# Attention and feed-forward on one core: two score groups per step, first transposes on TensorE, loads in smaller pieces and another order

## The chip, the core and the metric

The kernel runs on one core of a Trainium2 chip. The core has TensorE (PE; its weight loads are shown as PEld), VectorE (DVE), ScalarE (ACT), GpSimd (POOL) and SyncE (SP), and 16 DMA engines that all queues share. The metric is the device time of one execution in microseconds (us): the median of the runs, lower is better. The profile comes from one execution of its own.

## What is computed

Causal attention over 8 batches and 8 heads (S = 576 tokens, head size 64), with 16 extra "beacon" keys and values per head that every token may see; then a feed-forward layer without a nonlinearity on all 4608 tokens. Inputs and output are float32.

```python
k_all = concat([beacon_k, k], axis=2); v_all = concat([beacon_v, v], axis=2)
scores = q @ k_all.T / sqrt(64)              # causal mask on the non-beacon keys
a = softmax(scores);  attn = a @ v_all       # per batch and head
x = attn with heads side by side             # 4608 x 512
out = (((x @ w1) * (x @ w2)) @ w3) @ w_out   # w1, w2: 512x1024; w3: 1024x1024; w_out: 1024x512
```

## The kernel before

**Data.** All operands are float16 in SBUF; the loads on POOL's queue convert from float32. q, k and v of one batch come in five pieces of up to 128 tokens (`load_q`, `load_k`, `load_v`; the first piece of k and v holds the beacons) into two sets of buffers (batch number modulo 2). q and k are transposed by DMA transposes on SP's queue (`transpose_qk`, two per piece), so that the head dimension lies on the partitions. w3 and w_out are multiplied once into one matrix `Wt` (`fuse`), since nothing nonlinear lies between them; for it w3 is loaded into the unused second half of the buffer `xT` and transposed by eight DMA transposes on SP.

**Attention.** The unit is a pair of heads of one batch (32 pairs in all). Scores are computed transposed, keys on partitions, tokens on columns, and the causal upper part is left out. The blocks of a pair are packed into four groups of 368, 512, 384 and 400 columns per head (`GROUPS`), each for both heads in one PSUM tile `ps` of two banks; two such tiles exist. One step of the main loop (128 steps, 16 per batch) treats one group: `scores` on PE and the exponential on ACT straight into `pT`, `mask` on DVE (groups 0, 2 and 3), `values` on PE: p times v with a column of ones for the sum, then reciprocal and multiplication on DVE into `x16`. Values of token tiles 0 and 1 follow group 0, tiles 2 and 3 follow group 2, tile 4 follows group 3 (`DONE`). The scores run two steps ahead of the values. With the last pair of a batch each finished tile of `x16` goes through a DMA transpose on SP (line 326) into `xT`.

**Feed-forward.** Nine blocks of 512 tokens. `ff_ab` makes, for each of eight slices of 128 hidden units, two sums of four matmuls: the first is copied by ACT (`a_sb`, line 198), the second is multiplied with it on DVE (`gT`, line 200). `ff_out` multiplies gT with Wt, four sums of eight matmuls, which DVE scales (line 218) and SP stores. All PSUM tiles `pm` come from three banks. `stream` strings this together as a generator that gives one matmul at a time: block 0's `ff_ab`, then `fuse`, then `ff_out`, then the other blocks; 928 matmuls in all.

**Order.** Written by hand; every engine runs its own instructions in program order and waits by semaphores. Ahead of the loop: memsets, the mask constants, then on POOL's queue the loads of batch 0 (q, k, v), of w1 and w2 (2 DMAs), batch 1, w3 (4 DMAs), w_out; on SP's queue the transposes of batch 0, batch 1 and w3. In the loop each step issues scores(s+2), from step 20 on its share of FF matmuls (`emit_ff`), mask(s+1) and values(s). The first five steps of batch b issue the loads of batch b+1, steps 4 to 8 its transposes. What is left of the FF stream, 232 matmuls, follows the loop.

Of the kernel before, what the change touches and what calls it, by code (L numbers as in the profile page):

```python
# [23 lines left out]
GW = [368, 512, 384, 400]  # L24
GO = [400, 768, 1280, 0]
PW = 1664
# [11 lines left out]
DONE = [[0, 1], [], [2, 3], [4]]  # L38


@with_exitstack
def kernel(
# [13 lines left out]
    nc = tc.nc  # L56
# [19 lines left out]
    w3T = const.tile([P, NFT, DF], FP16, name="w3T")  # L76
# [11 lines left out]
    gp = ctx.enter_context(tc.tile_pool(name="gp", bufs=2))  # L88
    asb = ctx.enter_context(tc.tile_pool(name="asb", bufs=3))
# [6 lines left out]


    for i in range(NB2):
        nc.vector.memset(k16s[i][64:128, 4, :], 0.0)
        nc.vector.memset(vas[i][64:128, 4, :, :], 0.0)  # L100
    for m in (MA, MB):
        nc.gpsimd.memset(m, 1.0)
    for m, base in (
        (MA[:, 0:128], 0),
        (MA[:, 128:240], Nb),
        (MB[:, 0:128], 0),
        (MB[:, 128:256], 0),
    ):
        nc.gpsimd.affine_select(
            m,  # L110
            m,
            pattern=[[1, m.shape[1]]],
            compare_op=ALU.is_ge,
            fill=0.0,
            base=base,
            channel_multiplier=-1,
        )
    for i in range(NB2):
        for jt in range(NJT):
            n = P if jt < 4 else S + Nb - 4 * P  # L120
            nc.vector.memset(vas[i][0:n, jt, :, 64:65], 1.0)


    def load_q(b, c):
        rows = min(P, S - c * P)
        nc.gpsimd.dma_start(  # L126
            q16s[b % NB2][:rows, c, :].rearrange("s (h d) -> s h d", h=H),
            q[b, :, ds(c * P, rows), :].rearrange("h s d -> s h d"),
        )
# [23 lines left out]
    for c in range(NJT):  # L153
        load_q(0, c)
        load_k(0, c)
        transpose_qk(0, c)
    for c in range(NJT):
        load_v(0, c)
    for i, w in enumerate((moe_w1, moe_w2)):
        nc.gpsimd.dma_start(  # L160
            w12[:, :, ds(i * DF, DF)], w.rearrange("(t p) f -> p t f", p=P)
        )
    for c in range(NJT):
        load_q(1, c)
        load_k(1, c)
        transpose_qk(1, c)
# [3 lines left out]
    w316 = xT[:, :, ds(M // 2, 2 * DF)].rearrange("p a (c r) -> p a c r", c=2)  # L170
    for a in range(NKT):
        nc.gpsimd.dma_start(
            w316[:, a], moe_w3[ds(a * 2 * P, 2 * P)].rearrange("(c p) r -> p c r", p=P)
        )
    nc.gpsimd.dma_start(wo16, moe_w_out.rearrange("(t p) n -> p t n", p=P))
# [46 lines left out]
    def fuse():  # L222
        for kt in range(NFT):
            pm = psM.tile([P, DM], FP32, name="pm")
            for rt in range(NFT):
                nc.tensor.matmul(  # L226
                    pm,
                    w3T[:, rt, ts(kt, P)],
                    wo16[:, rt, :],
                    start=(rt == 0),  # L230
                    stop=(rt == NFT - 1),
                )
                if rt < NFT - 1:
                    yield
            nc.scalar.copy(Wt[:, kt, :], pm)
            yield
# [11 lines left out]
    def emit_ff(upto):  # L248
        nonlocal emitted
        while emitted < upto:  # L250
# [7 lines left out]
    NS = B * NT * 4  # L258
    pTs, pss, x16s = {}, {}, {}

    def scores(s):
        b, t, g = s // (4 * NT), (s // 4) % NT, s % 4
        if g == 0:
            pTs[s // 4] = ptp.tile([P, 2, PW], FP16, name="pT")
        ps = psS.tile([P, 2, 512], FP32, name="ps")
        pT = pTs[s // 4]
        qT, kT = qTs[b % NB2], kTs[b % NB2]
        for jt, q0, n, col in GROUPS[g]:
            for hh in range(2):
                nc.tensor.matmul(  # L270
                    ps[:, hh, ds(col, n)],
                    kT[ds(hh * 64, 64), t, ts(jt, P)],
                    qT[ds(hh * 64, 64), t, ds(q0, n)],
                )
        nc.scalar.activation(  # L275
            pT[:, :, ds(GO[g], GW[g])], ps[:, :, 0 : GW[g]], AF.Exp, scale=scale
        )

    def mask(s):
        g = s % 4  # L280
        pT = pTs[s // 4]
        if g == 1:
            return
        m = {0: MA, 2: MB, 3: MB[:, 0:80]}[g]
        n = m.shape[1]
        blk = pT[:, :, ds(GO[g], n)]
        nc.vector.tensor_tensor(  # L287
            blk, blk, m.unsqueeze(1).to_broadcast([P, 2, n]), ALU.mult
        )

    def values(s):
        b, t, g = s // (4 * NT), (s // 4) % NT, s % 4
        tiles = DONE[g]
        if not tiles:
            return
        pT = pTs[s // 4]
        va = vas[b % NB2]
        if t == 0 and g == 0:
            x16s[b] = xp.tile([P, NJT, DM], FP16, name="x16")
        x16 = x16s[b]  # L300
        ni = len(tiles)
        pv = psV.tile([P, 4, VS], FP32, name="pv")
# [10 lines left out]
        rd = sm.tile([P, 4], FP32, name="rd")  # L313
# [16 lines left out]
    S0 = 20  # L330
    FF_END = 7 * 96 + 64 - 40
    scores(0)
    scores(1)
    mask(0)
# [47 lines left out]
```

## Time and profile before

| | |
|---|---|
| runs | 377.56 us median of 3 (377.11 to 381.39) |
| profiled execution | 379.91 us, span 378.2 us |
| PE busy | 289.4 us, 77% of the span, 2592 matmuls |
| ACT, DVE, POOL busy | 155.6, 153.1, 115.9 us |
| PE busy in 0 to 100 us | 21.6 us |
| DMA | 46.31 MB, mean 122 GB/s |
| DMA queues' packet time, share of 16 engines' span | POOL's loads 72.9%, SP's transposes and stores 41.8% |

How to read the lines in the prediction. A line of the timeline or of the chain begins with its start and its length in us, then engine, line of the kernel, operation, output and input tiles, "x6" for six instructions merged, and in brackets the idle time before it and what ended that. A line of a group gives count, busy time in us and mean ns of one, then the idle time ahead of the group. Matmuls overlap and their ends are modelled, so a matmul's cost in a dense stretch is read from start to start, not from its length. In the rows of 40 slices a digit is the busy share of the slice in tenths. A DMA issue's line ends with the KB of each and the median us from issue to landing. PE at work does not always run at the same pace, though the granted clock is 1.00 in every stage of this profile: the durations show it.

### The profile page before, as it was taken

The page shows a single profiled execution, that of the slowest core. Times are in us where ns is not written, and L with a number is a line of the kernel's source. Part 1 is how long each engine was busy: PE and PEld are TensorE (multiplying, and loading weights), DVE is VectorE, ACT ScalarE, POOL GpSimd, SP SyncE. Part 2 cuts the span into 40 slices and gives each one's busy share as a digit, 9 for nine tenths or more (in the row PEclk, how much of TensorE's full clock was granted, in tenths as well). Part 3 has the DMA queues.
Part 4 walks back from the last instruction along what each step waited for, and adds up shares of the span by engine and source line. Part 5 has one row for each costly group of instructions (what it writes and reads, how often), then busy time and mean ns, then how long its engine had stood idle before and what let it go on. Part 6 is the DMA issues. An engine that isn't in the chain of part 4 may idle for free.

```text
span 378.2 us, 6634 instructions
## 1 busy us (share of the span) xinstructions
PE 289.4 (77%) x2592; PEld 145.5 (38%) x2592; DVE 153.1 (40%) x410; ACT 155.6 (41%) x209; POOL 115.9 (31%) x153
## 2 busy tenths in 40 slices
PE   0016620300079999999999999999999999999995
PEld 0004410200034554454554455454545554444442
DVE  1013510100025524555655565555565555443432
ACT  1025610300026566566466466456456556122130
POOL 9752642226200094068029208604700000000000
PEclk9999999999999999999999999999999999999999
DMA  9999999999990299989959999998995120420302
GB/s 61 152 175 194 153 150 188 172 128 155 156 142 16 42 130 144 198 89 160 187 107 139 164 168 107 156 170 126 167 162 104 52 86 12 80 83 0 113 0 111
DMA packets 192847, 46.31 MB, mean 122 GB/s; under 512 B 185137, under 2 KB 186161, under 8 KB 192817
## 3 DMA queue, kind: packets, MB, share of 16 engines
q0 software_dynamic: 118000, 19.67, 72.9%
q1 hardware_dynamic: 74816, 26.23, 41.8%
q8 instruction: 20, 0.33, 0.4%
q14 instruction: 11, 0.08, 0.1%
HBM read 39.32 MB, written 9.44 MB: 129 GB/s over the span
## 4 chain that ended last, share of the span: by engine, by line
PE 71%; DMA 21%; POOL 3%; SPq 3%; issue 1%; DVE 0%; POOLq 0%
PE pm L187 35%; PE pm L208 17%; PE ps L270 8%; PE pv L306 7%; DMA k<-in_k_dram 6%; DMA xT<-in_moe_w_dram 6%; DMA w<-in_moe_w_dram 5%; PE pm L226 4%; DMA va<-in_v_dram 3%; DMA xT<-x 2%; POOL q L126 2%; SPq L326 2%; SPq L177 1%; POOL k L135 1%; DVE ot L218 0%
## 5 line engine op out<-in xcount | busy, mean ns | idle before, releaser
L187 PE MATMUL pm<-xT,w 128*128 128x512 f16 x576 | 138.7, 383 | 36.0 <-DMA xT<-x 36.0
L275 ACT ACTIVATE pT<-ps 128x736 f16<-128x736 f32 (+3 forms) x128 | 110.1, 864 | 126.0 <-PE ps L270 124.3
L187 PEld LDWEIGHTS <-w 128*128 128x128 f16 x576 | 51.1, 98 | 98.1 <-issue 45.1
L270 PE MATMUL ps<-qT,kT 64*128 64x80 f16 (+3 forms) x704 | 48.7, 247 | 47.5 <-DMA kT<-k 40.3
L198 ACT ACTIVATE a_sb<-pm 128x512 f32<-128x512 f32 x72 | 42.9, 596 | 83.3 <-PE pm L187 81.4
L200 DVE TENSOR_TENSOR gT<-pm,a_sb 128x512 f16<-128x512 f32 x72 | 49.8, 692 | 60.9 <-PE pm L187 42.5
L135 POOL DMA_DIRECT2D va<-in_v_dram x40 | 34.6, 865 | 113.0 <-PE ps L270 100.1
L208 PE MATMUL pm<-Wt,gT 128*128 128x512 f16 x288 | 68.7, 380 | 0.0
L314 DVE RECIPROCAL rd<-pv 128x4 f32<-128x4 f32 (+1 forms) x96 | 16.9, 176 | 94.2 <-PE pv L306 93.7
L306 PEld LDWEIGHTS <-pT 128*128 128x128 f16 x960 | 44.4, 103 | 26.7 <-DVE x L315 4.9
L306 PE MATMUL pv<-va,pT 128*128 128x65 f16 x960 | 49.3, 201 | 1.3 <-DVE x L315 1.2
L270 PEld LDWEIGHTS <-kT 64*128 64x128 f16 x704 | 19.0, 100 | 65.3 <-DMA kT<-k 41.5
L135 POOL DMA_DIRECT2D k<-in_k_dram x40 | 34.6, 865 | 17.8 <-DMA va<-in_v_dram 8.9
L126 POOL DMA_DIRECT2D q<-in_q_dram x40 | 35.1, 877 | 13.2 <-DMA w<-in_moe_w_dram 4.0
L315 DVE TENSOR_TENSOR x<-pv,rd 128x256 f16<-128x256 f32 (+1 forms) x96 | 36.5, 380 | 3.4
L208 PEld LDWEIGHTS <-gT 128*128 128x128 f16 x288 | 25.7, 98 | 31.4 <-issue 3.5
L218 DVE TENSOR_SCALAR ot<-pm 128x512 f32<-128x512 f32 x36 | 24.9, 692 | 28.2 <-PE pm L208 28.1
L287 DVE TENSOR_TENSOR pT<-pT,MB 128x512 f16<-128x512 f16 x64 | 20.3, 325 | 16.7 <-ACT pT L275 16.6
L287 DVE TENSOR_TENSOR pT<-pT,MA 128x480 f16<-128x480 f16 x32 | 12.8, 399 | 17.4 <-ACT pT L275 17.4
L226 PE MATMUL pm<-wo,w3T 128*128 128x512 f16 x64 | 15.6, 381 | 0.0
L226 PEld LDWEIGHTS <-w3T 128*128 128x128 f16 x64 | 5.4, 98 | 6.7 <-issue 1.4
L139 POOL DMA_DIRECT2D k<-in_beacon_k_dram x8 | 4.2, 530 | 5.8 <-DMA q<-in_q_dram 4.7
(17 smaller groups left out, 19.1 us busy)
## 6 DMA issues: line engine op xcount, KB each, us to landing
out_dram<-ot SPq DMA_DIRECT2D x36, 256.0 KB, 2.3
q<-in_q_dram POOLq DMA_DIRECT2D x32, 128.0 KB, 7.6
k<-in_k_dram POOLq DMA_DIRECT2D x24, 128.0 KB, 7.3
va<-in_v_dram POOLq DMA_DIRECT2D x24, 128.0 KB, 8.2
w<-in_moe_w_dram POOLq DMA_DIRECT2D x2, 1024.0 KB, 15.7
xT<-in_moe_w_dram POOLq DMA_DIRECT2D x4, 512.0 KB, 18.7
wo<-in_moe_w_out_dram POOLq DMA_DIRECT2D x1, 1024.0 KB, 25.2
k<-in_k_dram POOLq DMA_DIRECT2D x8, 112.0 KB, 10.3
```

Source lines behind the costliest of these rows:

```text
L126: nc.gpsimd.dma_start(q16s[b % NB2][:rows, c, :].rearrange("s (h d) -> s h d", h=H), q[b, :, ds(c * P, rows), :].rearrange("h s d -> s h d"),)
L135: nc.gpsimd.dma_start(dst[ds(p0, rows)], src[b, :, ds(s0, rows), :].rearrange("h s d -> s h d"))
L187: nc.tensor.matmul(pm, w12[:, kt, ds(i * DF + kf * P, P)], xT[:, kt, ds(mc * 512, 512)], start=(kt == 0), stop=(kt == NKT - 1),)
L198: nc.scalar.activation(a_sb, pm, AF.Copy, scale=GS)
L200: nc.vector.tensor_tensor(gT[:, kf, :], pm, a_sb, ALU.mult)
L208: nc.tensor.matmul(pm, gT[:, kf, ts(mt, P)], Wt[:, kf, :], start=(kf == 0), stop=(kf == NFT - 1),)
L226: nc.tensor.matmul(pm, w3T[:, rt, ts(kt, P)], wo16[:, rt, :], start=(rt == 0), stop=(rt == NFT - 1),)
L270: nc.tensor.matmul(ps[:, hh, ds(col, n)], kT[ds(hh * 64, 64), t, ts(jt, P)], qT[ds(hh * 64, 64), t, ds(q0, n)],)
L275: nc.scalar.activation(pT[:, :, ds(GO[g], GW[g])], ps[:, :, 0 : GW[g]], AF.Exp, scale=scale)
L287: nc.vector.tensor_tensor(blk, blk, m.unsqueeze(1).to_broadcast([P, 2, n]), ALU.mult)
L306: nc.tensor.matmul(pv[:, 2 * n + hh, 0:65], pT[:, hh, ds(col, P)], va[:, jt, 2 * t + hh, 0:65], start=(jn == 0), stop=(jn == len(BLK[i]) - 1),
L315: nc.vector.tensor_tensor(x16[:, ds(tiles[0], ni), ds(t * P, P)].rearrange("p i (h d) -> p i h d", h=2), pv[:, 0 : 2 * ni, 0:64].rearrange ...
```

## The change

**Steps.** A step is now half a pair, two groups: 64 steps, eight per batch. `scores(s)` writes both groups into the two `ps` tiles; the exponentials (`exps`) and masks are functions of their own. `values` treats tiles 0 and 1 in the first half, tiles 2, 3 and 4 together in the second. The scores run one step ahead. In a step the order is scores(s+1), its first exponential, values(s), up to eight FF matmuls, the second exponential and first mask, the other FF matmuls, the second mask.

**Transposes.** Batch 0's q and k are transposed on PE against an identity (40 transposes of 128x128, five PSUM tiles, copied out by DVE and ACT), and w3 in `fuse` (64 transposes, eight copies on DVE, one slice ahead of its matmuls); their 18 DMA transposes are gone, and the buffer w3T with them. Batches 1 to 7 keep theirs.

**Loads.** Order on POOL's queue: batch 0's q and k, then v, w_out, w3 in eight pieces, w1 and w2 in four pieces each (256 columns), batch 1. Most memsets move to DVE; the mask constants are made behind the loads of q and k. From batch 1 on all loads of the next batch are issued in the batch's first step, the transposes in steps 1 to 5.

**FF stream.** `fuse` comes first, spread over steps 4 to 7 (16 matmuls each, with their transposes). Behind batch 0's last values come 60 matmuls of block 0 in one piece, then batch 1's DMA transposes and first scores; the other 36 of block 0 lie in batch 1; 536 matmuls lie in the 48 steps from batch 2 on; 232 follow the loop as before.

```diff
-    qTs = [const.tile([P, NT, S], FP16, name=f"qT_{i}") for i in range(NB2)]
+    qTs = [const.tile([P, NT, NJT * P], FP16, name=f"qT_{i}") for i in range(NB2)]
+    ident = const.tile([P, P], FP16, name="ident")
+    wp = ctx.enter_context(tc.tile_pool(name="wp", bufs=2))
...
+    nc.vector.memset(ident, 1.0)
+    nc.vector.memset(MA, 1.0)
+    nc.vector.memset(MB, 1.0)
+    load_q(0, 0)
+    load_k(0, 0)
+    load_q(0, 1)
+    nc.gpsimd.affine_select(
+        ident,
...
+    load_k(0, 1)
+    for c in range(2, NJT):
+        load_q(0, c)
+        load_k(0, c)
...
     for c in range(NJT):
         load_v(0, c)
-    for i, w in enumerate((moe_w1, moe_w2)):
-        nc.gpsimd.dma_start(
-            w12[:, :, ds(i * DF, DF)], w.rearrange("(t p) f -> p t f", p=P)
-        )
+    nc.gpsimd.dma_start(wo16, moe_w_out.rearrange("(t p) n -> p t n", p=P))
+    for kt in range(NFT):
+        nc.gpsimd.dma_start(w316[:, kt // 2, kt % 2], moe_w3[ts(kt, P), :])
+    for c in range(4):
+        for i, w in enumerate((moe_w1, moe_w2)):
+            nc.gpsimd.dma_start(
+                w12[:, :, ds(i * DF + c * 256, 256)],
+                w[:, ts(c, 256)].rearrange("(t p) f -> p t f", p=P),
+            )
...
-    for kt in range(NFT):
-        nc.sync.dma_start_transpose(w3T[:, :, ts(kt, P)], w316[:, kt // 2, kt % 2])
+    for c in range(NJT):
+        pt = psM.tile([P, 2, NT, P], FP16, name="pm")
+        for i, d16 in enumerate((q16s[0], k16s[0])):
+            for t in range(NT):
+                nc.tensor.transpose(pt[:, i, t, :], d16[:, c, ts(t, P)], ident)
+        nc.vector.tensor_copy(qTs[0][:, :, ts(c, P)], pt[:, 0])
+        nc.scalar.copy(kTs[0][:, :, ts(c, P)], pt[:, 1])
+
+    def fuse():
+        def w3_transposed(kt):
+            pt = psM.tile([P, NFT, P], FP16, name="pm")
+            for rt in range(NFT):
+                nc.tensor.transpose(pt[:, rt, :], w316[:, kt // 2, kt % 2, ts(rt, P)], ident)
+            wT = wp.tile([P, NFT, P], FP16, name="wT")
+            nc.vector.tensor_copy(wT, pt)
+            return wT
+
+        wT = w3_transposed(0)
+        for kt in range(NFT):
+            nxt = w3_transposed(kt + 1) if kt + 1 < NFT else None
+            pm = psM.tile([P, DM], FP32, name="pm")
+            for rt in range(NFT):
+                nc.tensor.matmul(pm, wT[:, rt, :], wo16[:, rt, :],
...
+            nc.scalar.copy(Wt[:, kt, :], pm)
+            wT = nxt
+            yield
...
     def stream():
+        yield from fuse()
         for mc in range(M // 512):
             gT = yield from ff_ab(mc)
-            if mc == 0:
-                yield from fuse()
             yield from ff_out(mc, gT)
...
+        b, t, half = s // (2 * NT), (s // 2) % NT, s % 2
...
+        pss[s] = []
+        for g in (2 * half, 2 * half + 1):
+            ps = psS.tile([P, 2, 512], FP32, name="ps")
+            pss[s].append(ps)
+            for jt, q0, n, col in GROUPS[g]:
...
+    def exps(s, j):
+        g = 2 * (s % 2) + j
+        pT = pTs[s // 2]
         nc.scalar.activation(
...
+        tiles = ([0, 1], [2, 3, 4])[half]
...
+        pv = psV.tile([P, 6, VS], FP32, name="pv")
...
+    NSB = 2 * NT
+    NS = B * NSB
+    LEFT = 40
+    n_first = 60
+    fill = [0] * NS
+    for s in range(4, 8):
+        fill[s] = 16
+    for s in range(NSB, 2 * NSB):
+        fill[s] = (96 - n_first) * (s - NSB + 1) // NSB - (96 - n_first) * (s - NSB) // NSB
+    rest, n = 6 * 96 - LEFT, NS - 2 * NSB
+    for s in range(2 * NSB, NS):
+        fill[s] = rest * (s - 2 * NSB + 1) // n - rest * (s - 2 * NSB) // n
...
     for s in range(NS):
-        b, r = s // 16, s % 16
-        if s + 2 < NS:
-            scores(s + 2)
-        if s >= S0:
-            emit_ff((FF_END * (s - S0 + 1)) // (NS - S0))
+        b, r = s // NSB, s % NSB
+        if s == NSB - 1:
+            emit_ff(fill[s])
+            values(s)
+            emit_ff(n_first)
+            for c in range(NJT):
+                transpose_qk(1, c)
+            scores(s + 1)
+            for j in range(2):
+                exps(s + 1, j)
+                mask(s + 1, j)
+            continue
         if s + 1 < NS:
-            mask(s + 1)
+            scores(s + 1)
+            exps(s + 1, 0)
         values(s)
+        k1 = min(8, fill[s])
+        emit_ff(k1)
+        if s + 1 < NS:
+            exps(s + 1, 1)
+            mask(s + 1, 0)
+        emit_ff(fill[s] - k1)
+        if s + 1 < NS:
+            mask(s + 1, 1)
         if 1 <= b < B - 1:
-            if r < NJT:
-                load_q(b + 1, r)
-                load_k(b + 1, r)
-                load_v(b + 1, r)
-            if 4 <= r < 4 + NJT:
-                transpose_qk(b + 1, r - 4)
+            if r == 0:
+                for c in range(NJT):
+                    load_q(b + 1, c)
+                    load_k(b + 1, c)
+                for c in range(NJT):
+                    load_v(b + 1, c)
+            if 1 <= r <= NJT:
+                transpose_qk(b + 1, r - 1)
```

More of the change, by code (lines that the diff above doesn't have):

```diff
@@ L36 @@
 ]
-DONE = [[0, 1], [], [2, 3], [4]]
 @with_exitstack
@@ L165 @@
         load_k(1, c)
-        transpose_qk(1, c)
     for c in range(NJT):
         load_v(1, c)
[L170 to L175, printed above, removed]
-    for kt in range(NFT):
-        nc.sync.dma_start_transpose(w3T[:, :, ts(kt, P)], w316[:, kt // 2, kt % 2])
+    for c in range(NJT):
[18 more added lines that the diff above has]
+            for rt in range(NFT):
+                nc.tensor.matmul(
+                    pm,
+                    wT[:, rt, :],
+                    wo16[:, rt, :],
+                    start=(rt == 0),
+                    stop=(rt == NFT - 1),
+                )
+                if rt < NFT - 1:
+                    yield
+            nc.scalar.copy(Wt[:, kt, :], pm)
+            wT = nxt
+            yield
     def ff_ab(mc):
@@ L220, in ff_out @@
             yield
[L222 to L236, printed above, removed]
     def stream():
+        yield from fuse()
         for mc in range(M // 512):
             gT = yield from ff_ab(mc)
-            if mc == 0:
-                yield from fuse()
             yield from ff_out(mc, gT)
@@ L246, with emit_ff @@
     emitted = 0
-    def emit_ff(upto):
+    def emit_ff(n):
         nonlocal emitted
-        while emitted < upto:
+        for _ in range(n):
             try:
@@ L291, in values @@
     def values(s):
[L292 to L296, printed above, removed]
+        b, t, half = s // (2 * NT), (s // 2) % NT, s % 2
+        tiles = ([0, 1], [2, 3, 4])[half]
+        pT = pTs[s // 2]
         va = vas[b % NB2]
-        if t == 0 and g == 0:
+        if t == 0 and half == 0:
             x16s[b] = xp.tile([P, NJT, DM], FP16, name="x16")
```

97 lines of the change are left out of this document (47 added, 50 removed).

## The prediction

> **What bounds the kernel now.** I read the page first: its sums, the span in 40 slices and the chain.
>
> ```profile
> span 378.2 us, 6634 instructions
> PE   0016620300079999999999999999999999999995
> DMA  9999999999990299989959999998995120420302
> ```
>
> A slice is 9.5 us. From the thirteenth on PE is full. Before that DMA is full and PE mostly empty. So there are two stages with two limits, and the first takes over a quarter of the span. DMA has full slices later too, with gaps between; how near it comes to a limit there is priced below. The chain of waits, in order of time, gives the joint between them and the pace at the end:
>
> ```profile
> 10.60 7.94 DMA k<-in_k_dram
> 18.82 17.32 DMA w<-in_moe_w_dram
> 50.18 21.01 DMA xT<-in_moe_w_dram
> 71.94 16.46 DMA k<-in_k_dram
> 99.13 7.19 DMA xT<-x
> 106.37 2.72 PE pm L187 x6
> ...
> 353.51 13.81 PE pm L187 x64
> 367.32 6.92 PE pm L208 x32
> ```
>
> The last piece of batch 0's k lands at 18.54. The feed-forward (FF) matmuls begin only at 106.37, because their input xT is queued on SP behind the eight transposes of w3, which wait for w3. At the end one FF matmul of 512 columns takes 13.81/64 = 0.216 us; PE is done at 374.24, and 4.0 us of drain follow. The whole kernel has 928 such matmuls (576 + 288 + 64), so 200.4 us.
>
> The price of attention in the full stage comes from the timeline of PE, one whole pair of heads (a "pair" below):
>
> ```profile
> 199.79 0.33 PE L270 MATMUL ps<-qT,kT 64*128 64x128 f16 x4
> 200.05 1.47 PE L187 MATMUL pm<-xT,w 128*128 128x512 f16 x6
> 201.36 0.59 PE L306 MATMUL pv<-va,pT 128*128 128x65 f16 x14
> 201.88 0.39 PE L270 MATMUL ps<-qT,kT 64*128 64x256 f16 x4
> 202.20 1.68 PE L187 MATMUL pm<-xT,w 128*128 128x512 f16 x7
> 203.72 0.47 PE L306 MATMUL pv<-va,pT 128*128 128x65 f16 x10
> 204.12 0.34 PE L270 MATMUL ps<-qT,kT 64*128 64x128 f16 x4
> 204.40 1.47 PE L187 MATMUL pm<-xT,w 128*128 128x512 f16 x6
> 205.70 0.34 PE L306 MATMUL pv<-va,pT 128*128 128x65 f16 x6
> 205.98 0.35 PE L270 MATMUL ps<-qT,kT 64*128 64x80 f16 x10
> 206.26 1.25 PE L187 MATMUL pm<-xT,w 128*128 128x512 f16 x5
> ```
>
> Start to next start is what a block costs: scores 0.26, 0.32, 0.28, 0.28 = 1.14 us; values 0.52, 0.40, 0.28 = 1.20 us; together 2.34 us per pair. As a check, from 106.37 to 325.88 there lie 704 FF matmuls (152.1) and 27 pairs (63.2), 215.3 against 219.5 measured: 4 us of small losses, some 1.4 of them the first six matmuls, which took 2.72 instead of 1.30. All PE work is then 200.4 + 32 x 2.34 = 275 us; the first stage is where there is time to win.
>
> **Part by part: the loads.**
>
> ```profile
> 2.36 1.02 POOL L126 DMA_DIRECT2D q<-in_q_dram  x1
> 12.83 2.67 POOL L135 DMA_DIRECT2D va<-in_v_dram  x3
> ```
> ```profile
> va<-in_v_dram POOLq DMA_DIRECT2D x3, 128.0 KB, 9.5
> ```
> ```profile
> q0 software_dynamic: 4023, 0.51, 136.8%
> q1 hardware_dynamic: 437, 0.11, 22.7%
> ```
> ```profile
> q0 software_dynamic: 2313, 2.26, 112.9%
> ```
> ```profile
> q0 software_dynamic: 7630, 0.96, 177.4%
> q1 hardware_dynamic: 1960, 0.47, 43.4%
> ```
>
> The last three fences are the DMA queues in the windows 4 to 10, 24 to 36 (nearly weights alone) and 140 to 150 us: packets, MB written, share. Splitting each window's time by the shares: q, k, v load at 0.51/5.15 = 99 GB/s at the start and at 0.96/8.0 = 120 later; weights, counting the small transposes beside them, near 205; transposes move at 0.47/2.0, about 240. A first batch of q and k (1.2 MB) loses its ten DMA transposes, which held 14% of the packets' time in the first window, 2 us up to 18.54; and POOL issues from about 0.8 instead of 2.36, since memsets go to DVE and the selects move behind (one select of ident, some 0.3 us, stays between). So k is whole at 18.54 - 1.55 - 2 = 15.0. Eight PE transposes of the last piece, their copies and hand-overs cost about 1.5: first scores at 16.5 instead of 18.5, and all five pieces are there then. Behind k, by the rates above: v 5 us to 20, wo (1.05 MB) 5 to 25, w3 1.25 per piece, first two pieces at 27.6 and the last at 35, w1 and w2 to 45.5, batch 1's q and k 10 us to 55.5.
>
> The pieces are 16 DMAs where 6 stood. Three v loads are issued in 2.67 us and each lands 9.5 us after its issue, so landings overlap; I cost the cutting at nothing, covered by the queue's backlog, and at the rival's price below if not. DMA: Bandwidth & Descriptors (the Trainium skill, section Anatomy of one DMA) gives about 2 us fixed per DMA and wants 1 MiB or more; taken one after the other, 16 pieces of 0.26 MB would by it cost 16 x 2.6 = 42 us as an estimate, and the row's overlap speaks against that here.
>
> **Batch 0.**
>
> ```profile
> 33.63 1.02 ACT L275 ACTIVATE pT<-ps 128x1024 f16<-128x1024 f32 x1 [0.22 <-PE ps L270]
> 33.78 0.73 PE L306 MATMUL pv<-va,pT 128*128 128x65 f16 x10 [0.19 <-DVE x L315]
> 38.10 1.02 ACT L275 ACTIVATE pT<-ps 128x1024 f16<-128x1024 f32 x1 [0.49 <-PE ps L270]
> ```
>
> Without FF work a pair takes 38.10 - 33.63 = 4.47 us, with PE slow (0.73 for a block that takes 0.47 in the full stage). The new steps let ACT run a little tighter; I take 4.25. Two pairs: 16.5 to 25. The fusion in the third and fourth pair waits for w3's first pieces: 28.6 with a hand-over. Then 64 matmuls 13.8, two pairs 4.1, 64 transposes of w3, one first copy out of PSUM 1.2.
>
> ```profile
> L270 PE MATMUL ps<-qT,kT 64*128 64x128 f16 x128 | 15.5, 239 | 25.8 <-DMA kT<-k 25.8
> ```
>
> No PE transpose stands in this trace. From below, 128 columns at 0.216/512 each are 0.054 us; from above, the 239 ns of this 128-column matmul, of which much is latency that neighbours overlap. Eight stand back to back each time, so I take 0.06: 3.8 us. The step ends at 28.6 + 22.9 = 51.5. The 40 transposes of q and k lie under the loads, but for the last eight.
>
> TensorE: Matmul & The Clock Gate (the Trainium skill, Part 4: PE-mode transpose) tells of about 275 ns per transpose within a kernel; 64 of them would be 17.6 us by that, 13.8 more than my sum, and that is a rival below.
>
> **The first FF block now waits for xT.** It needs batch 0 to row 512, hence its last tile.
>
> ```profile
> 93.06 7.29 SPq L326 DMA_TRANSPOSE xT<-x  x5
> ```
> ```profile
> xT<-x SPq DMA_TRANSPOSE x40, 2.5
> ```
>
> After the last values: DVE about 0.8, two SP issues ahead at 7.29/5 = 1.46, then 2.5 (median) to 7.19 (the row at 99.13, in a busy stretch): 6.2 to 10.9. The loads still run: I take 8. PE stands; queued behind are 60 FF matmuls and all of batch 1. To 59.5, and 60 matmuls with a slow start 13.0 + 1.4: 73.9. On SP batch 1's ten transposes come behind xT and behind their loads; the seventh, all that batch 1's first step needs, is issued near 65 and lands by 72, hidden by 2 us under the 60 matmuls. Batch 1 itself is light: four pairs 8.1 (with the saving below) and 36 FF 7.8 make 15.9 on PE, ACT's exponentials (the row of line 275 below) 16 x 0.864 = 13.8; with hand-overs 19. To 93. FF block 1 then needs rows to 1023, tile 3 of the batch that just ended: about 3.3 us of other work lies between, arrival 5 to 9.5: wait 4. Block 2 finds tile 3 of batch 2 about a step and a half old: 1.
>
> **Two groups per step, 48 steps from batch 2 on.** Scores' cost against columns (736 in 0.26, 1024 in 0.32) leaves 0.107 us per block; values (14, 10, 6 matmuls) leave 0.10. Two score blocks and one value block fewer per pair save 0.31, so 7.4 us in 24 pairs; the bounds are 0 and that. Against it stands a new wait. Both score buffers belong to one step, so the second group of the next step waits for this step's second exponential, which on ACT stands behind the a_sb copy of up to eight FF matmuls.
>
> ```profile
> L275 ACT ACTIVATE pT<-ps 128x736 f16<-128x736 f32 (+3 forms) x128 | 110.1, 864 | 126.0 <-PE ps L270 124.3
> L198 ACT ACTIVATE a_sb<-pm 128x512 f32<-128x512 f32 x72 | 42.9, 596 | 83.3 <-PE pm L187 81.4
> L200 DVE TENSOR_TENSOR gT<-pm,a_sb 128x512 f16<-128x512 f32 x72 | 49.8, 692 | 60.9 <-PE pm L187 42.5
> ```
>
> ```profile
> DMA  3739999999999999999999999999999097517005
> ```
>
> A step is scores 0.5, values 0.28 or 0.8, and 11.2 FF 2.4: 3.2 or 3.7 us. If the copy's matmul is the p-th of eight, the copy (0.6) and the exponential (0.9 to 1.0) end about 2.3 + 0.216p, or 3.1 + 0.216p in the long step; the next second group is due at 3.4, or 4.0. Early p cost nothing, p = 8 some 0.7 to 0.9; the mean over p is 0.2 and 0.3, in the two thirds of FF work that has such copies: 0.33 per pair. gT (0.69) ahead of the last mask does the same to the values, some 0.13. So 0.46 x 24 = 11 us; bounds 0 and every step in series, below. The last row is DMA from 196.4 to 228.6, one batch of before, in 40 slices: busy some 25 of 32.2 us. Eight new steps take 177.6/6 = 29.6 (sum below), still more than 25, so DMA stays behind PE. These 48 steps: 536 FF matmuls 115.8, 24 x 2.34 = 56.2, small losses 2, less 7.4, plus 11 = 177.6.
>
> **Sum:** 93 + 4 + 177.6 + 1 = 275.6; the last 232 FF matmuls, the same number as before, 50.1; drain 4.0: span 329.7. The profiled run of before took 379.91 for its span of 378.2, and its median of runs was 377.56, 0.6 below the span. So 329 us.
>
> **Rivals.** *Steps in series* (slower than before): if PE waited in each step for the copy (0.6), the exponential (0.93) and 0.4 of hand-overs, 1.9 x 48 = 91 in place of 11 gives 409. It decides from 1.4 us per step. Against it: two thirds of a step's time is FF that covers most of that chain. 4%. *The loads still bind*: small pieces at the small-packet rate, 5.2 MB of weights at 120 GB/s, would end at 64, batch 1's q and k at 74, its transposes at 88 instead of 72; behind 73.9 that is 14 late: 343. This is also where the fusion fails to fill batch 0. Against it, the weights' rate of before. 15%. *Dear transposes*: 64 x (0.239 - 0.06) = 11.5, so 341. For it, no row shows one. 13%. *All cover holds*: no step stall, quiet landings: 329 - 11 - 5 = 313. 14%. My forecast, with sizes off by some 10 us either way: 54%.
>
> A measurement here tells 2% (7.6 us) from nothing. Faster by more 0.95, within 0.02, slower 0.03. The range 312 to 348 takes in both dearer rivals and the better one, and leaves out their outer ends.
>
> **What will show it.** First scores near 16.5; the fusion's matmuls (line 226 now) starting near 29 with PE half full to 51; one PE gap of about 8 us before the first matmul of FF block 0 (line 187 now) near 60, a shorter one near 95; PE full from there with 0.2 to 0.5 us gaps at score blocks released by ACT; the last 232 matmuls from about 276. If the first FF matmul comes after 75, the loads or transposes were mispriced; if steps of 11 FF take over 4 us, the step was.

## The result, and the profile after

The changed kernel takes 346.73 us (median of 4 runs, 346.54 to 348.75). The kernel before, run beside it, takes 379.48 us (median of 4 runs, 377.11 to 382.59). The ratio is 0.9145, with a 95% interval of 0.9057 to 0.9232: faster. The forecast was 329 us, with 312 to 348 as the range. The profiled execution took 346.73 us for a span of 345.0.

The page of the changed kernel, its span and three rows of the 40 slices (8.6 us each; PEclk is the granted clock in tenths):

```profile
span 345.0 us, 6756 instructions
PE   2686980897943999599999989999999999999995
PEclk9998997699966899879999999999999999999999
DMA  9999999999999991999299999999833203301103
```

PE now works from the first slices on. Four dents remain, in slices 6, 11 and 12, and 16, and DMA is full until slice 14 and, but for slice 19, again from 16 to 27 (slices counted from 0). The clock row falls in and behind each dent; in the kernel before it showed nothing but nines. The chain of waits in order of time names what the dents wait for:

```profile
54.13 7.31 DMA xT<-x
61.58 5.01 PE pm L233 x12
...
92.74 6.82 DMA qT<-q
103.91 6.17 DMA xT<-x
110.21 4.36 PE pm L233 x11
...
140.23 5.83 DMA xT<-x
...
292.58 6.91 PE pm L254 x32
```

The four landings are DMA transposes: three of xT ahead of an FF block, one of batch 2's q. The timeline of PE through the first stage and one dense pair behind it (start, length, line, tiles, count, idle time before):

```profile
14.51 0.92 PE L300 MATMUL ps<-qT,kT 64*128 64x128 f16 x8
...
28.46 0.94 PE L203 MATMUL pm<-ident,xT 128*128 128x128 f16 x8 [2.64 <-DMA xT<-in_moe_w_dram]
...
30.54 2.62 PE L213 MATMUL pm<-wo,wT 128*128 128x512 f16 x8
33.01 0.61 PE L203 MATMUL pm<-ident,xT 128*128 128x128 f16 x8
33.45 1.89 PE L213 MATMUL pm<-wo,wT 128*128 128x512 f16 x8
...
49.83 0.89 PE L338 MATMUL pv<-va,pT 128*128 128x65 f16 x24
61.58 15.36 PE L233 MATMUL pm<-xT,w 128*128 128x512 f16 x60 [10.86 <-DMA xT<-x]
76.87 0.55 PE L300 MATMUL ps<-qT,kT 64*128 64x128 f16 x8
...
96.86 0.49 PE L300 MATMUL ps<-qT,kT 64*128 64x128 f16 x4 [2.75 <-DMA kT<-k]
99.70 0.61 PE L300 MATMUL ps<-qT,kT 64*128 64x256 f16 x4 [2.35 <-DMA qT<-q]
...
110.21 4.36 PE L233 MATMUL pm<-xT,w 128*128 128x512 f16 x11 [4.90 <-DMA xT<-x]
114.51 0.55 PE L300 MATMUL ps<-qT,kT 64*128 64x128 f16 x8
114.99 0.90 PE L338 MATMUL pv<-va,pT 128*128 128x65 f16 x24
115.73 2.54 PE L233 MATMUL pm<-xT,w 128*128 128x512 f16 x11
118.20 0.52 PE L300 MATMUL ps<-qT,kT 64*128 64x128 f16 x14
118.65 0.36 PE L338 MATMUL pv<-va,pT 128*128 128x65 f16 x6
118.85 2.54 PE L233 MATMUL pm<-xT,w 128*128 128x512 f16 x11
121.31 0.80 PE L300 MATMUL ps<-qT,kT 64*128 64x128 f16 x8
...
146.11 1.87 PE L233 MATMUL pm<-xT,w 128*128 128x512 f16 x4 [4.03 <-DMA xT<-x]
```

The stations of the forecast beside these:

| | forecast | measured |
|---|---|---|
| first scores | 16.5 | 14.5 |
| fusion starts (first transpose of w3) | 28.6 | 28.5 |
| end of batch 0 | 51.5 | 50.7 |
| FF block 0 starts, its 60 matmuls end | 59.5, 73.9 | 61.6, 76.9 |
| FF block 1 starts | 97 | 110.2 |
| last 232 matmuls start | 275.6 | 290.8 |
| span | 329.7 | 345.0 |

The last 232 start 8 x 0.216 ahead of the row at 292.58. Up to 76.9 the forecast is within 3 us everywhere. 13 of the 15 us that are missing in the end were lost before block 1 starts; from there to the last 232 it took 180.6 us for a forecast of 178.6. That these two agree is in part luck: waits for the second exponential came out smaller than forecast, waits for transposes and slow PE larger (below).

What SP did meanwhile (the timeline of its queue):

```profile
70.63 1.23 SPq L123 DMA_TRANSPOSE qT<-q  x1
72.05 1.20 SPq L124 DMA_TRANSPOSE kT<-k  x1
85.91 0.36 SPq L265 DMA_DIRECT2D out_dram<-ot  x1
86.36 1.22 SPq L123 DMA_TRANSPOSE qT<-q  x1
```

The first two are batch 2's first piece. Behind them in the program comes the store of block 0's first output tile (line 265), which has to be computed first; so SP stands for 12.7 us (from 73.25 to 85.91) with eight of batch 2's ten transposes behind the store. The piece that its first step lacks is issued at 92.74 and lands 6.8 us later.

### The profile page after: what moved, and what is told of

Its sections match the earlier page's. It is cut to its first block, busy times and chain, and to the rows that moved or that the text cites. A ratio compares the mean times of both kernels' runs of the same rounds, so it can differ in the third digit from the quotient of the medians.

```text
span 345.0 us, 6756 instructions
## 1 busy us (share of the span) xinstructions
PE 293.3 (85%) x2696; PEld 149.0 (43%) x2696; DVE 152.5 (44%) x363; ACT 153.4 (44%) x214; POOL 121.7 (35%) x162
## 4 chain that ended last, share of the span: by engine, by line
PE 60%; DMA 23%; POOL 8%; ACT 3%; issue 2%; DVE 2%; SPq 2%; POOLq 0%; DVEq 0%
PE pm L233 28%; PE pm L254 13%; PE pv L338 8%; DMA xT<-x 6%; PE ps L300 5%; DMA k<-in_k_dram 5%; DMA qT<-q 5%; PE pm L213 4%; DMA xT<-in_moe_w_dram 3%; DMA q<-in_q_dram 3%; POOL q L99 2%; POOL va L108 2%; POOL k L108 2%; ACT pT L309 2%; SPq L358 1%
## 5 line engine op out<-in xcount | busy, mean ns | idle before, releaser
L309 ACT ACTIVATE pT<-ps 128x736 f16<-128x736 f32 (+3 forms) x128 | 106.3, 863 | 43.2 <-PE ps L300 42.5
L233 PEld LDWEIGHTS <-w 128*128 128x128 f16 x576 | 55.2, 100 | 83.6 <-issue 27.2
L300 PE MATMUL ps<-qT,kT 64*128 64x80 f16 (+3 forms) x704 | 39.7, 237 | 13.4 <-ACT pT L309 6.4
L338 PE MATMUL pv<-va,pT 128*128 128x65 f16 x960 | 43.3, 198 | 2.7 <-DVE pT L321 2.6
L346 DVE RECIPROCAL rd<-pv 128x4 f32<-128x4 f32 x64 | 12.1, 189 | 74.3 <-PE pv L338 74.3
L338 PEld LDWEIGHTS <-pT 128*128 128x128 f16 x960 | 35.1, 100 | 13.2 <-issue 4.9
L254 PEld LDWEIGHTS <-gT 128*128 128x128 f16 x288 | 26.9, 98 | 29.6 <-issue 0.8
L347 DVE TENSOR_TENSOR x<-pv,rd 128x256 f16<-128x256 f32 x64 | 31.4, 491 | 2.6
L213 PE MATMUL pm<-wo,wT 128*128 128x512 f16 x64 | 15.7, 392 | 0.0
L222 ACT CAST Wt<-pm 128x512 f16<-128x512 f32 x8 | 4.7, 586 | 16.7 <-PE pm L213 16.7
L205 DVE COPY wT<-pm 128x1024 f16<-128x1024 f16 x8 | 5.5, 689 | 8.4 <-PE pm L203 8.4
```

The source lines that it names most:

```text
L213: nc.tensor.matmul(pm, wT[:, rt, :], wo16[:, rt, :], start=(rt == 0), stop=(rt == NFT - 1),)
L233: nc.tensor.matmul(pm, w12[:, kt, ds(i * DF + kf * P, P)], xT[:, kt, ds(mc * 512, 512)], start=(kt == 0), stop=(kt == NKT - 1),)
L254: nc.tensor.matmul(pm, gT[:, kf, ts(mt, P)], Wt[:, kf, :], start=(kf == 0), stop=(kf == NFT - 1),)
L300: nc.tensor.matmul(ps[:, hh, ds(col, n)], kT[ds(hh * 64, 64), t, ts(jt, P)], qT[ds(hh * 64, 64), t, ds(q0, n)],)
L309: nc.scalar.activation(pT[:, :, ds(GO[g], GW[g])], pss[s][j][:, :, 0 : GW[g]], AF.Exp, scale=scale)
L338: nc.tensor.matmul(pv[:, 2 * n + hh, 0:65], pT[:, hh, ds(col, P)], va[:, jt, 2 * t + hh, 0:65], start=(jn == 0), stop=(jn == len(BLK[i]) - 1),
```

## The experiments

Each run has runs of the kernel before beside it, whose medians lie between 377.48 and 380.00 us. Between two experiments a difference of 2 or 3 us is therefore no more than a hint; the traces say more.

**Batch 2's transposes ahead of the stores.**

```diff
+            if b == 1 and r == 0:
+                for c in range(NJT):
+                    transpose_qk(2, c)
-            if 1 <= r <= NJT:
+            if b > 1 and 1 <= r <= NJT:
                 transpose_qk(b + 1, r - 1)
```

> Batch 2's ten DMA transposes are put on SP's queue directly behind batch 1's, ahead of the stores of FF block 0; nothing else changes. Theory (SP's order): in the changed kernel SP stands from about 73.3 to 85.9 at the store of block 0's first output tile, with eight of batch 2's ten transposes behind it, and this late transpose delays batch 2's first scores (idle 2.8 + 2.4 us), through them batch 1's last values, their xT and FF block 1 (110.2). Without it block 1 starts between 101 and 105 and the time falls by 5 to 9 us, to 338 to 342. Rival (full DMA): the 16 engines are full from 50 to 93 with batch 2's and 3's loads, so the transposes land about as late wherever they stand: block 1 still at 108 or later, time 345 to 347.

Measured: 343.35 us (342.93 to 343.7), ratio 0.9066 (0.9006 to 0.9126). By the median both ideas missed: it gains more than the rival has it, less than the theory. The interval overlaps that of the changed kernel, so the trace has to show what changed. PE's timeline around the border of batches 1 and 2, and the transpose ahead of block 1 in this run's chain:

```profile
98.88 0.35 PE L338 MATMUL pv<-va,pT 128*128 128x65 f16 x6 [0.65 <-DVE pT L321]
107.67 4.53 PE L233 MATMUL pm<-xT,w 128*128 128x512 f16 x11 [8.43 <-DMA xT<-x]
```
```profile
99.92 7.61 DMA xT<-x
```

The idle time ahead of batch 2's scores is gone, so SP's order did cause it; but the wait for xT ahead of block 1 grew from 4.90 to 8.43 us. PE is ready 6 us earlier, but the transpose that block 1 needs is on its way only 4.0 us earlier (99.92 instead of 103.91) and lands after 7.61 us instead of 6.17. So block 1 starts 2.5 us earlier.

**Without the loads of batches 3 to 7.** On top of the edit above, loads are issued only in batch 1 (`if r == 0 and b == 1`); batches 3 to 7 then work on older data.

> The kernel with batch 2's transposes ahead of the stores, and without the loads of q, k and v of batches 3 to 7 (these batches work on what batches 1 and 2 left in the buffers, so that part of the computation is not of its own data). In the kernel with early transposes, block 1 still waited 8.4 us for xT, whose last needed transpose took 7.6 us from issue to landing. Theory (the transposes land late because the next batch's loads, let go by the same values, fill the 16 engines): the landing falls to 2.5 to 3.5 us, the wait to 3 to 4.5 us, block 2 waits 2 us or less, and the time falls by 7 to 11 us against the kernel with early transposes, to 332 to 337. Rival (SP's issue order and the transposes themselves make the wait): the landing stays over 6 us, the wait over 7, and the time within 3 us of 343.

Measured: 330.64 us (330.01 to 331.73), 12.7 less than with the loads; the theory holds, and a little more than it gave. PE's timeline at blocks 1 and 2:

```profile
101.36 3.93 PE L233 MATMUL pm<-xT,w 128*128 128x512 f16 x11 [2.78 <-DMA xT<-x]
...
133.24 1.02 PE L233 MATMUL pm<-xT,w 128*128 128x512 f16 x4 [0.38 <-DMA xT<-x]
```

And the DMA issues between 90 and 110 us, the kernel with early transposes first, then the one without later loads (median us from issue to landing):

```profile
xT<-x SPq DMA_TRANSPOSE x5, 7.4
```
```profile
xT<-x SPq DMA_TRANSPOSE x5, 2.4
```

The same five transposes land in 7.4 us beside the next batches' loads and in 2.4 without. In the changed kernel the values that release xT also release a load of v: POOL issues it (line 108) at 102.04 and 137.76, SP the last three transposes of xT at 102.63 and 138.31, so at both borders the two meet. How much of the landing time is due to v, and how much to the q and k issued around it, these runs don't separate.

**The order of FF matmuls changed instead.** Batch 1 keeps 4 matmuls of block 0; its second part goes into the first four steps of batch 2, and block 1 begins in the fifth.

```diff
-    for s in range(NSB, 2 * NSB):
-        fill[s] = (96 - n_first) * (s - NSB + 1) // NSB - (96 - n_first) * (s - NSB) // NSB
-    rest, n = 6 * 96 - LEFT, NS - 2 * NSB
-    for s in range(2 * NSB, NS):
+    fill[NSB] = 64 - n_first
+    for s in range(2 * NSB, 2 * NSB + 4):
+        fill[s] = 8
+    rest, s1 = 6 * 96 - LEFT, 2 * NSB + 4
+    n = NS - s1
+    for s in range(s1, NS):
...
```

> The changed kernel with another share of FF matmuls per step: batch 1 keeps only the last 4 of block 0's first part; the 32 of its second part go into the first four steps of batch 2 (8 each), and block 1 begins in the fifth step of batch 2, at 12.2 matmuls per step from there. Theory: what the changed kernel loses between 93 and 146 are waits at block borders, the transposes of batch 2 behind block 0's stores (5.1 us), xT for block 1 (4.9) and for block 2 (4.0), and some 3 to 4 us of slow PE behind each idle time; the new order puts 10 us of other work ahead of each, so block 1 and 2 start without idle time before them and the time falls by 9 to 14 us, to 333 to 338. Rival: the 16 DMA engines, full from 50 to 125, are the limit of this stretch; then the waits only move to the first scores of batch 2 or 3, and the time falls by 4 us at most, to 343 or more.

Measured: 331.84 us (330.75 to 333.32), ratio 0.8742 (0.8689 to 0.8795), 15 us below the changed kernel; the theory's sign and cause hold, its size was a little low. PE at the borders:

```profile
97.33 1.89 PE L254 MATMUL pm<-Wt,gT 128*128 128x512 f16 x8
...
111.06 2.76 PE L233 MATMUL pm<-xT,w 128*128 128x512 f16 x12
```

Block 1 starts at 111.06, no earlier than before, but with no idle time ahead of it, and 32 matmuls that the changed kernel did in batch 1 fill the time of the wait. No later block waits for xT either: the table of waits has one for it, 11.2 us, ahead of block 0. The DMA rival of this run is out.

**PE kept busy in the first gap.** 40 matmuls that nobody reads, between batch 0's last values and block 0.

```diff
             values(s)
+            pw = psM.tile([P, 512], FP32, name="pm")
+            for _ in range(40):
+                nc.tensor.matmul(pw, wo16[:, 0, 0:128], wo16[:, 0, :])
             emit_ff(n_first)
```

> 40 matmuls of 512 columns, whose result nobody reads, stand between batch 0's last values and the first 60 matmuls of FF block 0, in the gap of 10.9 us in which PE waits for xT; output unchanged. Theory (PE is slow after the gap): 40 x 0.216 to 0.43 = 8.6 to 11 us fit into the gap, block 0 starts at 61.6 to 62 as before, and its 60 matmuls take 13.0 instead of 15.3 us; that is 2 us less at that place, 344 to 345 in all if the waits behind it don't swallow it. Rival (the waits behind it are on SP and DMA, not on PE): the 60 matmuls end 2 us earlier, but batch 2's first scores come when their transposes do, and the time stays 346 to 347.

Measured: 346.12 us (345.21 to 349.81). That is the rival's number, but the runs are spread over both ranges. PE's timeline:

```profile
50.43 8.79 PE L386 MATMUL pm<-wo 128*128 128x512 f16 x40
61.16 13.11 PE L233 MATMUL pm<-xT,w 128*128 128x512 f16 x60 [1.93 <-DMA xT<-x]
...
98.21 0.61 PE L300 MATMUL ps<-qT,kT 64*128 64x256 f16 x4 [5.69 <-DMA qT<-q]
```

The 60 matmuls do take 13.1 instead of 15.3 us, so idle time costs PE speed behind it. But batch 2's scores then wait 5.69 for qT instead of 2.35 at that place, a wait that PE does not set. Block 1 starts at 109.45 instead of 110.21: of the 2.2 us 0.8 are left there, too little to tell from nothing in the runs.

**The second exponential ahead of the FF matmuls.**

```diff
-        k1 = min(8, fill[s])
+        k1 = 0 if s >= 2 * NSB else min(8, fill[s])
```

> From batch 2 on the second exponential of a step stands ahead of the step's FF matmuls in the program, so that on ACT no a_sb copy is ahead of it. Theory (waits for the second exponential cost 5 to 7 us over the 48 steps): they go, and the time falls by 4 to 7 us, to 340 to 343. Rival (the copy behind the exponential now holds PSUM tiles of the FF sums, or the mask waits elsewhere): idle time moves to the FF matmuls, and the time stays within 2 us of 347.

Measured: 341.21 us (340.78 to 343.38), ratio 0.8998 (0.8944 to 0.9052), 5.5 us less than the changed kernel, within the theory's range. In the table of waits PE's time for `ps <- ACT pT` falls (the changed kernel's row, then this one's: us, times, longest):

```profile
PE ps L300 <- ACT pT L309: 6.4, 12, 1.0
```
```profile
PE ps L300 <- ACT pT L309: 3.1, 5, 1.0
```

The five that remain all lie ahead of batch 2, so from batch 2 on the wait is gone. The table lists 3.3 us of it, less than the 5 to 7 of the theory. The rest of the 5.5 us is not in this row; the dense stretch shows shorter delays that are not listed, such as the score block at 121.31 in the changed kernel, which takes 0.73 us to the next start instead of 0.48.

**The two-group steps alone,** in the kernel before, with its loads, transposes and FF order.

```diff
-    S0 = 20
...
+    S0 = 10
     FF_END = 7 * 96 + 64 - 40
...
+            n = (FF_END * (s - S0 + 1)) // (NS - S0) - emitted
```

> The kernel before with its loads, its DMA transposes and its FF order, but with the two-group steps of the changed kernel (64 steps, FF from step 10 on at an even rate). Theory (prediction's sum for the step): 27 pairs gain 0.3 us each on PE, 8 us, and lose 0.3 to 0.46 to waits for the second exponential, 8 to 12 us: 374 to 384, no difference that can be measured, so that the whole gain of the change comes from the first stage. Rival A (switches saved, waits small): 369 to 373. Rival B (steps in series): 390 or more.

Measured: 370.44 us (367.59 to 373.06), ratio 0.978 (0.9694 to 0.9866): rival A, a gain of 7 us. The interval lies below 1 but reaches across 0.98, so that there is a gain is clear, and that it is 2% is not. In its profile the FF work starts at

```profile
102.00 5.28 PE L187 MATMUL pm<-xT,w 128*128 128x512 f16 x12 [32.69 <-DMA xT<-x]
```

and 265.8 us of the span of 367.8 remain from there, against 378.2 - 106.37 = 271.8 in the kernel before: some 6 us come from the full stage, and 4.4 from the earlier start (the two profiled executions differ by 10.4, the medians by 7). The 6 us are 0.22 per pair of the 0.42 that PE saves (below). Part of what is missing is a slow start, twelve FF matmuls in 5.21 us instead of 2.59, and waits for the exponential, 1.4 us in all; the rest was not traced. The waits are shorter than the 3.3 us of the changed kernel. Its steps hold 13 FF matmuls instead of 11, so there is more cover for the second exponential; that this is the reason is argued, not shown.

**Loads in large pieces,** in the new order: w3 in four, w1 and w2 in one each.

```diff
-    for kt in range(NFT):
-        nc.gpsimd.dma_start(w316[:, kt // 2, kt % 2], moe_w3[ts(kt, P), :])
+    for a in range(NKT):
+        nc.gpsimd.dma_start(
+            w316[:, a], moe_w3[ds(a * 2 * P, 2 * P)].rearrange("(c p) r -> p c r", p=P)
+        )
...
```

> The order of the loads is kept, but w3 comes in four pieces instead of eight and w1, w2 in one each instead of four. Theory (cutting costs nothing, landings overlap): the fusion's first slices wait some 1 to 2 us longer, all else as in the changed kernel: 346 to 349. Rival (a fixed cost of 2 us per DMA in series): ten DMAs fewer make the loads end up to 20 us earlier, FF block 0 and batch 1 come earlier, and the time falls by 5 us or more.

Measured: 347.9 us (345.9 to 350.17); no difference from the changed kernel can be told. The fusion's matmuls start 1.8 us later:

```profile
30.53 1.89 PE L203 MATMUL pm<-ident,xT 128*128 128x128 f16 x16 [4.98 <-DMA xT<-in_moe_w_dram]
32.35 3.11 PE L213 MATMUL pm<-wo,wT 128*128 128x512 f16 x8
```

So the cutting costs nothing and brings next to nothing. No run takes back the order of the loads, the fusion ahead of block 0 or the PE transposes of w3 one by one, so what each of them brings is not shown. DMA: Bandwidth & Descriptors (the Trainium skill, section Anatomy of one DMA) gives 2 us fixed per DMA; ten transfers fewer in a full queue did not show that here.

**Batch 0's q and k by DMA transposes again.**

```diff
-        pt = psM.tile([P, 2, NT, P], FP16, name="pm")
...
-        nc.scalar.copy(kTs[0][:, :, ts(c, P)], pt[:, 1])
+        transpose_qk(0, c)
```

> The changed kernel with one part undone: batch 0's q and k transposed by ten DMA transposes on SP again instead of 40 transposes on PE. Theory (prediction's first stage: the first scores are set by k's landing, and the DMA transposes cost their own landing beside loads that fill the engines): first scores at 20 to 24 instead of 14.5, the second step's last piece at 27 to 31, the fusion begins at 36 to 42 instead of 30.5, and the time rises by 6 to 12 us, to 353 to 359. Rival (the fusion waits for w3 until 28 anyway, and a gap behind it swallows the rest): the time rises by 3 us at most, to 350.

Measured: 351.88 us (350.91 to 354.6), ratio 0.9307 (0.9240 to 0.9375), 5 us above the changed kernel: between the two, just under the theory. The rows of its PE:

```profile
16.98 0.49 PE L294 MATMUL ps<-qT,kT 64*128 64x128 f16 x4 [16.98 <-DMA kT<-k]
...
28.05 0.51 PE L294 MATMUL ps<-qT,kT 64*128 64x80 f16 x10 [3.77 <-DMA kT<-k]
...
38.05 1.90 PE L207 MATMUL pm<-wo,wT 128*128 128x512 f16 x8 [0.44 <-DVE wT L199]
```

First scores come 2.5 us later, sooner than the theory had them, the last piece at 28 and the fusion 7.5 us later. In the two profiled executions nothing of that is swallowed: FF block 0 starts 7.8 us later (69.38) and the spans are 352.9 and 345.0. The profiled execution is the slowest of this kernel's four; the medians differ by 5.

**Gains put together.** On the version with the other FF order: second exponential first, and 16 of the fusion's matmuls (12 instead of 16 in each of steps 4 to 7) moved into the gap ahead of block 0; then the same with 32 in the gap; then the first of these without the loads of batches 3 to 7.

```diff
-        fill[s] = 16
+        fill[s] = 12
...
-            emit_ff(n_first)
+            emit_ff(16 + n_first)
```

> The kernel with block 0's second part later, with the second exponential ahead of the FF matmuls from batch 2 on, and with 12 instead of 16 fusion matmuls in each of steps 4 to 7, the other 16 (with their transposes) in the gap behind batch 0's last values, where PE waits 11.2 us for xT. Theory (the three waits are separate and add up): 5 us from the exponential, 3.5 to 4.5 from the gap: 322 to 325. Rival (batch 1's transposes, next on SP, set the end of that stretch): the gap's gain is lost at batch 1's first scores, 326 to 328.

> As the run with 16 fusion matmuls in the gap, but with 8 in each of steps 4 to 7 and 32 in the gap (7 us plus 4 sets of eight transposes, 1.8). Theory: block 0's 60 matmuls start when xT is there, which is 3 to 4 us earlier still, but batch 1's first scores then meet transposes that are not there before 73: 320 to 324. Rival: batch 1's transposes take it all, the time is that of the other run within 1.5 us.

> The run with 16 fusion matmuls in the gap, without the loads of q, k and v of batches 3 to 7 (these batches work on older data). In the run with the loads the gains of 5 us (second exponential first) and 4 us (gap filled) did not show, and DMA was full up to 230 us. Theory (DMA has become the limit, its transposes and loads being late from batch 3 on): the time falls to 318 to 322, that is by the 9 us that were missing and a little more. Rival (the gains are lost on PE, ACT or in SP's order): the time stays at 327 or more.

Measured: 331.3 us (329.64 to 332.53), 333.4 (332.91 to 333.5) and 324.09 (323.1 to 325.52). For the first, theory and rival both missed (322 to 328); the second lies further from the first than its rival has it, though the intervals of the ratios overlap (0.8763 and 0.8805, each 0.005 to 0.007 either way); the third lies between its theory and its rival. The gains do not add up: 331.3 is the time of the FF order alone, and more fusion in the gap is no better. DMA's row of slices (8.2 us) in the first of the three, two waits from its PE, and the rows of the table of waits for qT, first of the kernel with the FF order alone, then of this one:

```profile
DMA  9999999999999999999999999999451202302103
```
```profile
118.05 0.39 PE L300 MATMUL ps<-qT,kT 64*128 64x256 f16 x4 [3.72 <-DMA qT<-q]
...
151.17 0.39 PE L300 MATMUL ps<-qT,kT 64*128 64x256 f16 x4 [1.87 <-DMA qT<-q]
```
```profile
PE ps L300 <- DMA qT<-q: 1.5, 1, 1.5
```
```profile
PE ps L300 <- DMA qT<-q: 6.1, 3, 3.7
```

DMA has no gap left up to 230 us, and the scores of batches 3 and 4 wait for their transposes. With kT (0.6 and 1.5 us) the waits for q's and k's transposes rise from 2.1 to 7.6 us (11.1 in the run with 32), which takes back over half of the 9 us that were expected. Without the later loads the time falls by 7.2 us. No run takes the loads from the kernel with the FF order alone, so how much of these 7 us belongs to the two gains, and where the rest went, stays open. Fastest of the kernels that do the whole computation are the first of these three and the one with the FF order alone, about 331.5 us, 15 below the changed kernel.

## Why the prediction was right, and where its sizes were off

Direction and range hold. The mechanism holds too: the first stage was bound by loads and by SP's transposes, the new order lets fusion and attention of batch 0 run inside it, and the FF work starts at 61.6 instead of 106.4. The gain was forecast as 48 us (from 377.56 to 329) and is 33 (from 379.48 to 346.73). The measured time lies 18 us above the forecast, more than the "some 10 us either way" for its sizes, and 1.3 us below the end of the range. The range had that room for two dearer rivals, dear transposes (341) and loads that still bind (343), and neither happened as described; that the range held is therefore in part luck. The rival that all cover holds (313) is out by the waits below.

**The loads.** Right in rate and order. The last piece of k landed at 13.8 (issued at 9.94, 3.9 us to landing) for a forecast of 15.0, and first scores came 2 us earlier than said; w3's first two pieces were there at 28.5 and 29.7 for a forecast of 27.6, and PE's first stage ended within 1 us of the sum. The cutting was rightly costed at nothing (the run with large pieces). The estimate "2 us" for DMA transposes beside the first loads was good: with them the last piece of k, issued at 9.95, took 6.3 us to landing.

**PE transposes.** 0.06 us each was forecast; eight in a row take 33.45 - 33.01 = 0.44, so 0.055, near the bound from below, and the rival of dear transposes is out. The 275 ns of TensorE: Matmul & The Clock Gate (the Trainium skill, Part 4: PE-mode transpose) is not what a transpose in a row of them costs here.

**Two groups per step.** The saving of 0.31 per pair was of the right kind and too small. In the changed kernel scores take 0.48 and 0.45, values 0.74 and 0.20, together 1.87; eleven FF matmuls ahead of scores take 2.47 instead of 11 x 0.216 = 2.38, so 0.09 more per step: 2.05 per pair. The 2.34 of the kernel before leaves such a remainder out. Its pair from 199.79 ends with

```profile
207.88 0.33 PE L270 MATMUL ps<-qT,kT 64*128 64x128 f16 x4
```

so it takes 8.09 us, less 26 FF matmuls (5.62) 2.47: the 0.13 beyond 2.34 stand among the sum's small losses. PE saves 0.42 per pair. This fits a cost for each change between the two kinds of matmul, with half as many changes per pair. The waits for the second exponential were forecast at 11 us, masks included; moving it ahead gives back 5.5, of which the table of waits lists 3.3. The waits listed lie between 0.25 and 0.7 us, so the 0.7 to 0.9 for p = 8 was near; the sum of 11 was about twice too large. The rival of steps in series is out: the steps alone made the kernel before faster.

**The step that failed** is the one on block borders: "To 93. FF block 1 then needs rows to 1023 ... wait 4. Block 2 ... 1", and ahead of it "I take 8" for xT. The forecast was 8 + 0 + 4 + 1 = 13 us of waits; measured are 10.86 + 5.10 + 4.90 + 4.03 = 24.9 (5.10 is 2.75 + 2.35 at batch 2's first scores). Three errors lie in it:

- Batch 2's DMA transposes had no term at all. The sum followed SP's queue to batch 1's transposes and stopped there; behind them stand block 0's stores, and behind those the rest of batch 2's. It cost 5.1 us of idle time, and, since the last values of batch 1 come behind these scores in PE's program, it pushed xT and block 1 back as well. Batch 3's cost another 1.6 us of idle time, also without a term.
- xT's landing was taken between the quiet 2.5 and the busy 7.2, nearer to quiet the later the border. The three that set the waits took 7.31, 6.17 and 5.83 us, all near the busy end. The runs with and without later loads show 7.4 and 2.4 for the same transposes, so the loads in flight make the difference.
- After each wait PE is slow for some microseconds. The sum had 1.4 us for it once, behind block 0. Measured there are 15.3 - 13.1 = 2.2 (the run with the busy gap); at block 1 eleven matmuls take 4.30 instead of 2.47, and behind the waits of batch 2 and block 2 PE is slow again (five in 2.24 instead of 1.08, four in 1.80 instead of 0.86).

**"So DMA stays behind PE"** compared busy time per batch with the time of eight steps, 25 against 29.6. The throughput was enough for the 48 steps to come out within 2 us of the sum, but beside full engines every transpose lands late, and that was not in the comparison. The rival that the loads still bind had the right resource with the wrong place: weights came at nearly the rate of the sum (the second piece of w3 was 2 us late); what DMA delayed were transposes at block borders, from batch 2 on. Once the borders were covered, taking away later loads still gained 7 us, so DMA held the kernel back from there.

## What to carry to other kernels

When a change fills an idle stage, follow each queue past the last step that was moved, to the first wait of the next stage: a store that waits for compute holds up every prefetch issued behind it on the same queue (12.7 us here). Where one event releases both a result that is needed at once and the next bulk load, take the loaded landing time, not the median, or put other work between. Put a number on successive waits together: removing the first returns only what the second does not take (here 2.5 of 5.1 us).

## What the runs showed of the hardware

- The landing time of a DMA transpose on SP's queue depends on what POOL's queue has in flight: five of them took 7.4 us (median) beside the loads of q, k and v, 2.4 without.
- PE behind an idle gap of 10.9 us needs 15.3 us for 60 matmuls that take 13.1 when it was kept at work, and the profile's clock row shows it (7 and 6 tenths in the slices of the gap and behind it). The row alone is no proof of full pace: in the kernel before it is all nines, though ten value matmuls took 0.73 us in the first stage and 0.47 in the full one.
- A change between score matmuls (64 rows) and the others costs about 0.1 us on PE, as worked out from blocks of different sizes: 0.107 per score block of before, 0.09 on the FF matmuls ahead of the scores after.
- Eight PE transposes of 128x128 in a row took 0.44 us, start to next start, 0.055 each.
